# Dealing the second matmul out between single f tiles, transposes behind f tiles 13 and 14, plain tap products and a new ramp, in a fused dynamic convolution and feed-forward kernel

## Chip, cores and metric

One core of one Trainium2 chip. The metric is the device time of one execution in microseconds (us), lower is better. Every run is recorded at a granted clock of 0.993 to 1.000.

## The reference, cut to what matters

```python
w = softmax(weight_gen, axis=-1)                     # (8, 4096, 8 heads, 7 taps)
x_pad = concat([zeros(B, 6, 192), x], axis=1)
out = einsum('bshk,bskhg->bshg', w, windows(x_pad))  # causal, 7 taps, 24 channels a head
h = out.reshape(32768, 192) @ w_in                   # 192 -> 2048
y = (h - tanh(h)) @ w_out                            # 2048 -> 192, float32
```

## The kernel before: the parts that matter

32 blocks (n) of 1024 tokens. For each, GpSimd multiplies the seven taps; an accumulating DMA adds some of the products to others; TensorE (PE) transposes what is left against an identity and sums it in PSUM (`conv_sums`); PE then runs 16 f tiles of the first matmul (`gemm1`; an f tile is 128 of the 2048 hidden columns), ScalarE takes tanh, VectorE (DVE) subtracts, and PE runs the second matmul of the block before (`out_block`, 16 pairs of row tiles for each 128 tokens; a pair is two matmuls on 64 rows each, which overlap in the trace: they start 20 ns apart, pairs 82 ns apart, and each is recorded as 243 ns). `ph`, `pc` and `obank`, which PE writes to, are tiles in PSUM.

```python
for n in range(1, NTOT):
    for p in range(J):                       # J = 8
        more = n < NTOT - 1
        if more and p == 6:
            break
        gemm1(n, 2 * p)
        ...
        gemm1(n, 2 * p + 1)
        ...                                  # softmax pieces of block n + 3
        out_block(n, p, ahead)
        if p == 0 and 1 < n < NTOT - 2:
            products(n + 2, behind=last_sub[0])      # taps of block n + 2, paced
        if p == 0 and n + 3 < NTOT and n not in LATE:
            load_x(n + 3)                            # LATE = (1, ..., 6)
    ...
    gemm1(n, 12); gemm1(n, 13)
    ...                                      # transposes of n + 1 mixed into the pairs of p = 6
    conv_out(n + 1, ((0, 1),), pcs)          # ScalarE
    ...
    conv_out(n + 1, ((2,),), pcs, nc.vector) # DVE
    if n + 3 < NTOT:
        softmax_norm(n + 3, pcs[0][:, 0])    # DVE: copy, scale
    gemm1(n, 14); gemm1(n, 15)
    out_block(n, 7, FILL)
    if n in LATE:
        load_x(n + 3, last_conv[0])          # behind the transposes
```

In `products` each tap is an instruction of its own, the DMA sum follows tap 5 (of taps 0 to 6), and the products lie as [channel third, token, head, 8], so that the transposes load packed columns.

The softmax here doesn't subtract the row's maximum and nothing guards it: scores larger than these inputs give would overflow.

## Time and profile before

| | before |
|---|---|
| median (three runs at the start) | 754.81 us (753.72 to 756.43) |
| busy share PE, DVE, GpSimd, ScalarE | 97%, 93%, 89%, 83% |
| one steady block | 22.49 us |
| loads of x, landing | 1344 KB each, 9.3 us |
| DMA sums, landing | 1024 KB each, 8.8 us |

A busy share averages over stages; what counts is who waits.

### The profile page before, as it was taken

What the parts mean: (1) busy time and instruction counts of PE and PEld (TensorE: products, weight loads), DVE (VectorE), ACT (ScalarE), POOL (GpSimd) and SP (SyncE); (2) the same over time, 40 slices, a digit from 0 to 9 for tenths busy, and PEclk for the clock granted to TensorE, in tenths of its full rate; (3) what the DMA queues carried; (4) which work ended last, traced back from release to release, by engine and by line L of the source; (5) the groups of instructions that cost most, each with busy time, mean ns of one, the idle gap of its engine ahead of it and who ended that gap; (6) DMA issues with size and microseconds to landing.
All of it is one profiled execution on the core that took longest, in us unless ns stands there. A gap on an engine that the chain in (4) does not pass through costs nothing.

```text
span 751.8 us, 32359 instructions
## 1 busy us (share of the span) xinstructions
PE 732.1 (97%) x14800; PEld 577.5 (77%) x14800; DVE 695.5 (93%) x740; ACT 625.3 (83%) x840; POOL 670.5 (89%) x264
## 2 busy tenths in 40 slices
PE   3899999999999999999999999999999999999997
PEld 2477878877777778777777778777878777877777
DVE  7999999999999999999999999999999999998893
ACT  4888888888888888888888888888888888888883
POOL 8999999999999999999999999999999999999000
PEclk9999999999999999999999999999999999999999
DMA  8936444465556665555666544666544566542312
GB/s 229 213 79 172 152 149 111 107 186 171 158 161 155 186 184 126 136 151 160 176 186 172 125 130 149 171 184 186 121 125 148 168 186 173 121 115 62 79 45 86
DMA packets 25943, 110.82 MB, mean 147 GB/s; under 512 B 4703, under 2 KB 9551, under 8 KB 21838
## 3 DMA queue, kind: packets, MB, share of 16 engines
q1 hardware_dynamic: 14718, 77.03, 28.3%
q0 software_dynamic: 11088, 31.72, 24.9%
q8 instruction: 115, 1.88, 1.0%
q14 instruction: 22, 0.18, 0.1%
HBM read 54.52 MB, written 25.17 MB: 106 GB/s over the span
## 4 chain that ended last, share of the span: by engine, by line
PE 94%; DVE 4%; DMA 1%; ACT 0%; issue 0%; DVEq 0%
PE obank L358 44%; PE ph L320 43%; PE pc L277 6%; DVE gt L334 2%; PE po L395 1%; DMA x_t<-in_x_dram 1%; DVE odd L224 0%; DMA wg_t<-in_weight_gen_dram 0%; DVE even L224 0%; DVE zsum L160 0%; DVE obank L199 0%; ACT convT L295 0%; ACT e_t L146 0%; DVE obank L188 0%; DVE zr L169 0%
## 5 line engine op out<-in xcount | busy, mean ns | idle before, releaser
L334 DVE TENSOR_TENSOR gt<-ph,th 128x1024 bf16<-128x1024 f32 x512 | 602.5, 1220 | 33.0 <-ACT th L333 30.0
L333 ACT ACTIVATE th<-ph 128x1024 f32<-128x1024 f32 x512 | 497.5, 1022 | 69.4 <-PE ph L320 68.0
L358 PE MATMUL obank<-w_out,gt 64*128 64x192 bf16 x7936 | 412.5, 243 | 0.1
L358 PEld LDWEIGHTS <-gt 64*128 64x128 bf16 x7936 | 357.4, 94 | 55.7 <-issue 0.2
L320 PE MATMUL ph<-convT,w_in 64*128 64x512 bf16 x3072 | 384.9, 378 | 4.8 <-DVE gt L334 2.8
L224 POOL TENSOR_TENSOR even<-x_t,wsm 128x1536 bf16<-128x1536 f32 x93 | 287.6, 3092 | 12.3 <-DVE gt L334 12.1
L224 POOL TENSOR_TENSOR odd<-x_t,wsm 128x1536 bf16<-128x1536 f32 x93 | 287.3, 3089 | 0.0
L320 PEld LDWEIGHTS <-w_in 64*128 64x128 bf16 x3072 | 174.6, 94 | 101.6 <-issue 11.6
L377 ACT ACTIVATE out_sb<-obank 128x192 f32<-128x192 f32 x248 | 82.3, 332 | 35.0 <-PE obank L358 30.5
L224 POOL TENSOR_TENSOR last<-x_t,wsm 128x1536 bf16<-128x1536 f32 x32 | 106.6, 3333 | 0.0
L277 PE MATMUL pc<-ident,even 64*128 64x64 bf16 x2256 | 62.8, 191 | 0.3 <-DVE even L224 0.2
L277 PEld LDWEIGHTS <-even 64*128 64x128 bf16 x2304 | 59.7, 96 | 1.2 <-issue 0.5
L241 POOL DMA_DIRECT2D even<-odd x30 | 36.1, 1205 | 9.3 <-POOL odd L224 9.3
L277 PE MATMUL pc<-ident,last 64*128 64x64 bf16 x752 | 27.2, 191 | 9.3 <-POOL last L224 9.2
L303 ACT ACTIVATE convT<-pc 128x1024 bf16<-128x1024 f32 (+1 forms) x33 | 32.6, 992 | 2.8 <-PE pc L277 2.8
L277 PEld LDWEIGHTS <-last 64*128 64x128 bf16 x768 | 23.2, 96 | 9.6 <-POOL last L224 9.2
L160 DVE TENSOR_REDUCE zsum<-e_t 128x32 f32<-128x224 f32 (+1 forms) x61 | 23.7, 388 | 3.0 <-ACT e_t L146 3.0
L146 ACT ACTIVATE e_t<-wg_t 128x448 f32<-128x448 f32 x32 | 18.5, 578 | 6.7 <-DMA wg_t<-in_weight_gen_dram 6.7
L301 DVE CAST convT<-pc 128x512 bf16<-128x512 f32 x30 | 20.7, 690 | 3.6 <-PE pc L277 1.9
L169 DVE RECIPROCAL zr<-zsum 128x32 f32<-128x32 f32 (+1 forms) x58 | 20.3, 350 | 0.0
L199 DVE TENSOR_TENSOR wsm<-e_t,pc 128x448 f32<-128x448 f32 x28 | 17.4, 622 | 2.9
L277 PE MATMUL pc<-ident,odd 64*128 64x64 bf16 x416 | 14.7, 198 | 1.1 <-POOL odd L224 0.7
(29 smaller groups left out, 77.5 us busy)
## 6 DMA issues: line engine op xcount, KB each, us to landing
x_t<-in_x_dram SPq DMA_DIRECT2D x31, 1344.0 KB, 9.3
even<-odd POOLq DMA_DIRECT2D x25, 1024.0 KB, 8.8
out_dram<-out_sb SPq DMA_DIRECT2D x31, 768.0 KB, 6.9
wg_t<-in_weight_gen_dram SPq DMA_DIRECT2D x32, 224.0 KB, 10.0
even<-odd POOLq DMA_DIRECT2D x5, 768.0 KB, 7.1
x_t<-in_x_dram SPq DMA_DIRECT2D x1, 768.0 KB
w_out<-in_moe_w_out_dram POOLq DMA_DIRECT2D x1, 768.0 KB, 10.3
out_dram<-out_sb SPq DMA_DIRECT2D x4, 192.0 KB, 1.9
```

Of the source, the lines that this page charges most:

```text
L160: nc.vector.reduce_sum(out=zsum_of[n][:, j0 * H : j1 * H], in_=e_of[n][:, j0:j1].rearrange("p j h k -> p (j h) k"), axis=AX.X,)
L169: nc.vector.reciprocal(zr_of[n][:, j0 * H : j1 * H], zsum_of[n][:, j0 * H : j1 * H])
L224: mul = eng.tensor_mul(dst[k][:, :, j0:j1].rearrange("p c j h g -> p j h c g"), x_t[:, k + j0 : k + j1, :].rearrange("p j (h c g) -> p j h ...
L241: nc.gpsimd.dma_start(out=even[:].rearrange("p i c j h g -> p (i c j h g)")[:, 0:acc], in_=odd[:].rearrange("p i c j h g -> p (i c j h g)" ...
L277: nc.tensor.matmul(pc[r][:, col : col + R] if home else pc[:, r, col : col + R], lhsT=prods[c][gi][r * R : (r + 1) * R, c, 2 * j : 2 * j + ...
L301: eng.tensor_copy(out, pc[:, :, 0:cols].rearrange("p r (cj t) -> p r cj t", t=R))
L303: last_conv[0] = nc.scalar.activation(out=out, in_=pc[:, :, 0:cols].rearrange("p r (cj t) -> p r cj t", t=R), func=ACT.Copy,)
L320: nc.tensor.matmul(ph[:, r, :], lhsT=w_in[r * R : (r + 1) * R, c, f * P : (f + 1) * P], rhs=convT[r * R : (r + 1) * R, c, :], start=(c == ...
L333: last_act[0] = nc.scalar.activation(out=th[:], in_=ph_f, func=ACT.Tanh)
L334: last_sub[0] = nc.vector.tensor_sub(gt[:], ph_f, th[:])
L358: mm = nc.tensor.matmul(po[:, 0:D], lhsT=g_of[n][f][r * R : (r + 1) * R, col : col + P], rhs=w_out[r * R : (r + 1) * R, f, :], start=(r == ...
L377: last_act[0] = nc.scalar.activation(out=out_sb[:, j, :], in_=po[:, 0:D], func=ACT.Copy)
```

## The change

Its intent: keep PE fed at finer grain, take the last eviction from DVE, use fewer GpSimd instructions, need fewer transposes, and close the gap between the first two blocks. The diff, cut to its core:

```diff
-    PART = (2, 3, 4, 5, 6)
+    PART = tuple(range(2,5))
+    SUM_FIRST = tuple(range(5,32))
 ...
-        even = ppool.tile([P, NPAIR, NC, J, H, GC], BF16, name="even")
-        ... odd, last; one instruction per tap
+        pr = ppool.tile([P, K, J, D], BF16, name="pr")
+            mul(nc.gpsimd, 0, 2)
+            mul(nc.gpsimd, 2, 6)
+            if n in SUM_FIRST:
+                dma_sum(pr, 0, 3, 3, 6)
+            mul(nc.gpsimd, 6, K)
 ...
-    (conv_sums) lhsT=prods[c][gi][r * R : (r + 1) * R, c, 2 * j : 2 * j + 2]   # packed
+    (conv_sums) ... "p j (u c) -> p c (j u)" [:, c]                             # step of 3
 ...
+    STEADY = dict(pairs=(4, 12, 0, 16, 0, 16, 0, 16, 0, 6, 10, 6, 10, 8, 8, 16),
+                  t1=(14, 8), t2=(13, 0), scale=14, sums=(2, 5))
+    X_AT = 7
+        for f in range(NFT):
+            gemm1(n, f)
 ...
-                products(n + 2, behind=last_sub[0])
+                    products(n + 2)                      # f == 1, no pace
-            if p == 0 and n + 3 < NTOT and n not in LATE:
-                load_x(n + 3)
+            if f == X_AT and n + 3 < NTOT:
+                load_x(n + 3, last_sub[0])
 ...
+                    pc = transposes(n + 1, chunks)       # in one run; ScalarE evicts
 ...
-    softmax_norm_ramp(2)              # GpSimd scales block 2's weights
+    softmax_norm_ramp(2, obank[0])    # DVE scales them
```

More of the change, by code (lines that the diff above doesn't have):

```diff
@@ L43 @@
     NC = D // R
-    GC = G // NC
-    NPAIR = K // 2
-    ACC = NPAIR * J * D - J * R
     PLAIN = (0, 1)
-    PART = (2, 3, 4, 5, 6)
-    assert S % TOK == 0 and D % R == 0 and H * GC == R and F % P == 0
+    PART = tuple(range(2,5))
+    TWO_SUMS = tuple(())
+    SUM_FIRST = tuple(range(5,32))
+    SCALE_TWICE = True
+    assert S % TOK == 0 and D % R == 0 and F % P == 0
     assert NFT == 2 * J, "one token block of the second matmul per pair of f tiles"
@@ L77 @@
     prods_of = {}
+    to_sum = {}
     conv_of = {}
@@ L174, in softmax_norm, with finish, softmax_norm_ramp @@
         zr_v = bank[:, 512 - J * H : 512]
-        nc.vector.tensor_copy(zr_v, zr_of[n][:])
-        scale(nc.vector, wsm[:], e_of[n], zr_v)
-        wsm_of[n] = (wsm, None, None, None)
-    def softmax_norm_ramp(n, bank=None):
+        nc.vector.reciprocal(zr_v, zsum_of[n][:])
+        def finish():
+            scale(nc.vector, wsm[:], e_of[n], zr_v)
+            wsm_of[n] = (wsm, None, None, None)
+        return finish
+    def softmax_norm_ramp(n, bank):
         softmax_sum(n)
         wsm = softmax_tile()
-        if bank is None:
-            softmax_recip(n)
-            wsm_of[n] = (wsm, None, e_of[n], zr_of[n])
-            return
         zr_v = bank[:, 512 - J * H : 512]
         nc.vector.reciprocal(zr_v, zsum_of[n][:])
-        if n == 0:
+        if n == 2:
             scale(nc.vector, wsm[:], e_of[n], zr_v)
-        else:
-            zr_of[n] = wgpool.tile([P, J * H], FP32, name="zr")
-            nc.vector.tensor_copy(zr_of[n][:], zr_v)
+            wsm_of[n] = (wsm, None, None, None)
+            return
         wsm_v = bank[:, 0 : J * H * K].rearrange("p (j h k) -> p j h k", j=J, h=H)
+        if n == 0 and SCALE_TWICE:
+            scale(nc.vector, wsm[:], e_of[n], zr_v)
         scale(nc.vector, wsm_v, e_of[n], zr_v)
-        wsm_of[n] = (wsm, wsm_v, None if n == 0 else e_of[n], zr_of.get(n))
+        if n == 1 or not SCALE_TWICE:
+            nc.scalar.activation(
+                out=wsm[:].rearrange("p j h k -> p (j h k)"),
+                in_=wsm_v.rearrange("p j h k -> p (j h k)"),
+                func=ACT.Copy,
+            )
+        wsm_of[n] = (wsm, wsm_v, None, None)
     def scale(eng, wsm, e_t, zr):
@@ L203, in scale, with dma_sum, products @@
         )
-    def products(n, taps=None, sums=None, hooks={}, behind=None):
+    def dma_sum(pr, k0, k1, src0, src1, step=1):
+        nc.gpsimd.dma_start(
+            out=pr[:, k0:k1].rearrange("p k j d -> p k (j d)"),
+            in_=pr[:, src0:src1:step].rearrange("p k j d -> p k (j d)"),
+            accum_op=mybir.AluOpType.add,
+            max_dma_last_dim=2 * J * D,
+        )
+    def products(n, taps=None, sums=None, hooks={}):
         x_t = x_of.pop(n)
@@ L210, in products @@
             scale(nc.gpsimd, wsm[:], e_t, zr[:])
-        even = ppool.tile([P, NPAIR, NC, J, H, GC], BF16, name="even")
-        odd = ppool.tile([P, NPAIR, NC, J, H, GC], BF16, name="odd")
-        last = ppool.tile([P, NC, J, H, GC], BF16, name="last")
-        dst = {}
-        for i in range(NPAIR):
-            dst[2 * i] = even[:, i]
-            dst[2 * i + 1] = odd[:, i]
-        dst[K - 1] = last[:]
-        if -1 in hooks:
-            hooks[-1]()
-        for eng, k, j0, j1 in taps or [(nc.gpsimd, k, 0, J) for k in range(K)]:
-            w = wsm_v if eng is nc.vector else wsm[:]
-            mul = eng.tensor_mul(
-                dst[k][:, :, j0:j1].rearrange("p c j h g -> p j h c g"),
-                x_t[:, k + j0 : k + j1, :].rearrange("p j (h c g) -> p j h c g", h=H, c=NC),
-                w[:, j0:j1, :, k : k + 1]
-                .rearrange("p j h (k o) -> p j h k o", o=1)
-                .to_broadcast([P, j1 - j0, H, NC, GC]),
-            )
-            if k == 0 and behind is not None:
-                order(mul, behind, "pace")
-            if j1 == 1:
-                first_halo[0] = mul
-            if (k, n in PART) in ((3, True), (K - 2, False)) and n not in PLAIN:
-                acc = 2 * J * D if n in PART else ACC
-                nc.gpsimd.dma_start(
-                    out=even[:].rearrange("p i c j h g -> p (i c j h g)")[:, 0:acc],
-                    in_=odd[:].rearrange("p i c j h g -> p (i c j h g)")[:, 0:acc],
-                    accum_op=mybir.AluOpType.add,
-                    max_dma_last_dim=4096,
-                )
-            if k in hooks:
-                hooks[k]()
@@ new lines, in products, with mul @@
+        pr = ppool.tile([P, K, J, D], BF16, name="pr")
+        x_v = x_t[:]
+        step = x_v.ap[0]
+        def mul(eng, k0, k1, j0=0, j1=J):
+            w = wsm_v if eng is nc.vector else wsm[:]
+            nj = j1 - j0
+            return eng.tensor_mul(
+                pr[:, k0:k1, j0:j1, :].rearrange("p k j (h g) -> p k (j h) g", h=H),
+                bass.AP(
+                    tensor=x_v.tensor,
+                    offset=x_v.offset + (k0 + j0) * D,
+                    ap=[step, [D, k1 - k0], [G, nj * H], [1, G]],
+                ),
+                w[:, j0:j1]
+                .rearrange("p j h (k o) -> p k (j h) o", o=1)[:, k0:k1]
+                .to_broadcast([P, k1 - k0, nj * H, G]),
+            )
@@ L250, in products, with parts @@
+        def parts(*ks):
+            return [[pr[:, k] for k in ks]] * NC
+        if taps is not None:
+            for eng, k0, k1, j0, j1 in taps:
+                m = mul(eng, k0, k1, j0, j1)
+                if j1 == 1:
+                    first_halo[0] = m
+                if k0 in hooks:
+                    hooks[k0]()
+            prods_of[n] = parts(*sums)
+            return
         if n in PLAIN:
-            prods_of[n] = [[dst[k] for k in (sums or range(K))]] * NC
+            mul(nc.gpsimd, 0, 3)
+            mul(nc.gpsimd, 3, 5)
+            mul(nc.gpsimd, 5, K)
+            prods_of[n] = parts(*range(K))
@@ L252, in products @@
         elif n in PART:
-            prods_of[n] = [[dst[4], even[:, 0], even[:, 1], dst[5], last[:]]] * NC
-        else:
-            groups = [last[:]] + [even[:, i] for i in range(NPAIR)]
-            prods_of[n] = [
-                groups + ([odd[:, NPAIR - 1]] if c == NC - 1 else []) for c in range(NC)
-            ]
+            mul(nc.gpsimd, 0, 2)
+            mul(nc.gpsimd, 2, 4)
+            dma_sum(pr, 0, 2, 2, 4)
+            mul(nc.gpsimd, 4, K)
+            prods_of[n] = parts(4, 5, 6, 0, 1)
+        else:
+            mul(nc.gpsimd, 0, 2)
+            second_sum(n - 1)
+            mul(nc.gpsimd, 2, 6)
+            if n in SUM_FIRST:
+                dma_sum(pr, 0, 3, 3, 6)
+            mul(nc.gpsimd, 6, K)
+            if n not in SUM_FIRST:
+                dma_sum(pr, 0, 3, 3, 6)
+            if n in TWO_SUMS:
+                to_sum[n] = pr
+                prods_of[n] = parts(0, 1)
+            else:
+                prods_of[n] = parts(6, 0, 1, 2)
+            if n == NTOT - 1:
+                second_sum(n)
@@ L260, in conv_sums, with second_sum @@
+    def second_sum(n):
+        if n in to_sum:
+            dma_sum(to_sum.pop(n), 0, 2, 2, K, 4)
     def conv_sums(n, parts, pcs, home=None):
@@ L278, in conv_sums @@
                                 pc[r][:, col : col + R] if home else pc[:, r, col : col + R],
-                                lhsT=prods[c][gi][
-                                    r * R : (r + 1) * R, c, 2 * j : 2 * j + 2
-                                ].rearrange("p j h g -> p (j h g)"),
+                                lhsT=prods[c][gi][r * R : (r + 1) * R, 2 * j : 2 * j + 2].rearrange(
+                                    "p j (u c) -> p c (j u)", c=NC
+                                )[:, c],
                                 rhs=ident[r * R : (r + 1) * R, r * R : (r + 1) * R],
@@ L337 @@
     LAST = (NTOT - 1) * J
-    LEAD = 5
-    FILL, AHEAD = 2, 1
-    LATE = (1, 2, 3, 4, 5, 6)
     half = {}
     out_of = {}
-    def gemm2(i, f0=0, f1=NFT, between=lambda f: None):
-        ops = []
-        for r, blk in ((0, i), (1, i - 1)):
-            if not 0 <= blk < LAST:
-                continue
-            n, j = divmod(blk, J)
-            if r == 0 and f0 == 0:
-                half[blk] = obank[blk % 2]
-            ops.append((r, n, j, half[blk]))
-        for f in range(f0, f1):
-            for r, n, j, po in ops:
-                col = (j % 2) * HT + (j // 2) * P
-                mm = nc.tensor.matmul(
-                    po[:, 0:D],
-                    lhsT=g_of[n][f][r * R : (r + 1) * R, col : col + P],
-                    rhs=w_out[r * R : (r + 1) * R, f, :],
-                    start=(r == 0 and f == 0),
-                    stop=(r == 1 and f == NFT - 1),
-                )
-                if r == 1 and f == 0 and i in (1, LAST):
-                    order(mm, probe[0] if i == 1 else last_act[0], "row tiles in one bank")
-            between(f)
-        if i > 0 and f1 == NFT:
-            blk = i - 1
-            n, j = divmod(blk, J)
-            po = half.pop(blk)
-            if j == 0:
-                out_of[n] = opool.tile([P, J, D], FP32, name="out_sb")
-            out_sb = out_of[n]
-            last_act[0] = nc.scalar.activation(out=out_sb[:, j, :], in_=po[:, 0:D], func=ACT.Copy)
-            if j == J - 1:
-                out_of.pop(n)
-                g_of.pop(n)
-                nc.sync.dma_start(
-                    out=out[n * TOK : (n + 1) * TOK, :].rearrange("(p j) e -> p j e", p=P),
-                    in_=out_sb[:],
-                )
@@ new lines, in out_stream @@
+    def out_stream():
+        for i in range(LAST + 1):
+            ops = []
+            for r, blk in ((0, i), (1, i - 1)):
+                if not 0 <= blk < LAST:
+                    continue
+                n, j = divmod(blk, J)
+                if r == 0:
+                    half[blk] = obank[blk % 2]
+                ops.append((r, n, j, half[blk]))
+            for f in range(NFT):
+                for r, n, j, po in ops:
+                    col = (j % 2) * HT + (j // 2) * P
+                    mm = nc.tensor.matmul(
+                        po[:, 0:D],
+                        lhsT=g_of[n][f][r * R : (r + 1) * R, col : col + P],
+                        rhs=w_out[r * R : (r + 1) * R, f, :],
+                        start=(r == 0 and f == 0),
+                        stop=(r == 1 and f == NFT - 1),
+                    )
+                    if r == 1 and f == 0 and i in (1, LAST):
+                        order(mm, probe[0] if i == 1 else last_act[0], "row tiles in one bank")
+                if f == NFT - 1 and i > 0:
+                    store_out(i - 1)
+                yield
@@ new lines, in store_out @@
+    def store_out(blk):
+        n, j = divmod(blk, J)
+        po = half.pop(blk)
+        if j == 0:
+            out_of[n] = opool.tile([P, J, D], FP32, name="out_sb")
+        out_sb = out_of[n]
+        last_act[0] = nc.scalar.activation(out=out_sb[:, j, :], in_=po[:, 0:D], func=ACT.Copy)
+        if j == J - 1:
+            out_of.pop(n)
+            g_of.pop(n)
+            nc.sync.dma_start(
+                out=out[n * TOK : (n + 1) * TOK, :].rearrange("(p j) e -> p j e", p=P),
+                in_=out_sb[:],
+            )
@@ L386, in gemm2_last, with out_pairs @@
+    pairs = out_stream()
+    def out_pairs(m):
+        for _ in range(m):
+            next(pairs)
     def gemm2_last(j, f0=0, f1=NFT):
@@ L426, with load_w_in @@
     FA = 7 * P
-    def w_in_rows(c, f0, f1):
-        src = moe_w_in[c * GC : c * GC + 1, f0:f1]
-        return bass.AP(
-            tensor=src.tensor, offset=src.offset, ap=[[G * F, H], [F, GC], [1, f1 - f0]]
-        )
-    def load_w_in(f0, f1, behind=None):
-        for c in range(NC):
-            dma = nc.gpsimd.dma_start(out=w_in[0:R, c, f0:f1], in_=w_in_rows(c, f0, f1))
-            if c == 0 and behind is not None:
-                order(dma, behind, "order of the loads")
+    def load_w_in(c0, c1, f0, f1, behind=None):
+        src = moe_w_in[c0 : c0 + 1, f0:f1]
+        dma = nc.gpsimd.dma_start(
+            out=w_in[0:R, c0:c1, f0:f1],
+            in_=bass.AP(
+                tensor=src.tensor,
+                offset=src.offset,
+                ap=[[NC * F, R], [F, c1 - c0], [1, f1 - f0]],
+            ),
+        )
+        if behind is not None:
+            order(dma, behind, "order of the loads")
     def rest_of_w_in():
-        load_w_in(FA, F)
+        load_w_in(0, NC, FA, F)
     V, G_ = nc.vector, nc.gpsimd
@@ L448 @@
     softmax_exp(0)
-    load_w_in(0, FA, last_exp[0])
+    for c in range(NC):
+        load_w_in(c, c + 1, 0, FA, last_exp[0] if c == 0 else None)
     softmax_norm_ramp(0, obank[0])
@@ L454 @@
         taps=[
-            (G_, 6, 0, J),
-            (V, 5, 1, J),
-            (V, 4, 2, J),
-            (V, 5, 0, 1),
-            (V, 4, 0, 2),
-            (G_, 0, 0, J),
-            (V, 3, 0, J),
-            (V, 2, 0, J),
-            (G_, 1, 0, J),
+            (G_, 6, 7, 0, J),
+            (V, 5, 6, 1, J),
+            (V, 4, 5, 2, J),
+            (V, 5, 6, 0, 1),
+            (V, 4, 5, 0, 2),
+            (G_, 0, 1, 0, J),
+            (V, 3, 4, 0, J),
+            (V, 2, 3, 0, J),
+            (G_, 1, 2, 0, J),
         ],
@@ L479 @@
         1,
-        taps=[(V, 0, 0, J), (V, 1, 0, J)] + [(G_, k, 0, J) for k in range(2, K)],
-        hooks={4: load_w_out},
+        taps=[(V, 0, 1, 0, J), (V, 1, 2, 0, J), (G_, 2, 5, 0, J), (G_, 5, 7, 0, J)],
+        sums=range(K),
+        hooks={2: load_w_out},
     )
@@ L494 @@
     load_x(3)
-    for p in range(J):
-        gemm1(0, 2 * p)
-        gemm1(0, 2 * p + 1)
-        if p == 3:
+    PER = 4 * JH
+    EARLY, THIRD = ((7, 3), (9, 1), (11, 7)), 13
+    for f in range(NFT):
+        gemm1(0, f)
+        if f == 1:
+            softmax_exp(3)
+        if f == EARLY[0][0]:
             pcs = []
             sums = conv_sums(1, ((0, 1),), pcs, obank)
-        if p == 0:
-            softmax_exp(3)
-        if 3 <= p <= 6:
-            some(sums, (3 if p == 3 else 1) * 4 * JH)
@@ L507 @@
-    some(sums, K * 4 * JH)
-    conv_out(1, ((0, 1),), pcs)
-    conv(1, (2,))
-    def out_block(n, p, f0=0, f1=NFT, between=lambda f: None):
-        gemm2((n - 1) * J + p, f0, f1, between)
-    for n in range(1, NTOT):
-        for p in range(J):
-            more = n < NTOT - 1
-            if more and p == 6:
-                break
-            gemm1(n, 2 * p)
-            ahead = AHEAD if p == 0 and n > 1 else 0
-            if ahead:
-                out_block(n, p, 0, ahead)
-            gemm1(n, 2 * p + 1)
+        for at, groups in EARLY:
+            if f == at:
+                some(sums, groups * PER)
@@ new lines @@
+        if f == EARLY[-1][0]:
+            conv_out(1, ((0, 1),), pcs)
+        if f == THIRD:
+            pcs = []
+            for _ in conv_sums(1, ((2,),), pcs, obank):
+                pass
+            conv_out(1, ((2,),), pcs)
+    STEADY = dict(pairs=(4, 12, 0, 16, 0, 16, 0, 16, 0, 6, 10, 6, 10, 8, 8, 16), t1=(14, 8), t2=(13, 0), scale=14, sums=(2, 5))
+    FIRST = dict(pairs=(4, 12, 0, 16, 1, 15, 0, 16, 0, 16, 0, 13, 3, 0, 16, 16), t1=(15, 2), t2=(11, 10), scale=15, sums=(1, 2, 3, 4, 8, 10))
@@ L524, with transposes @@
+    X_AT = 7
+    def transposes(n, chunks):
+        pcs = []
+        for _ in conv_sums(n, (chunks,), pcs):
+            pass
+        conv_out(n, (chunks,), pcs)
+        return pcs[0]
+    for n in range(1, NTOT):
+        more = n < NTOT - 1
+        finish = None
+        plan = FIRST if n == 1 else STEADY
+        for f in range(NFT):
+            gemm1(n, f)
             if n == 1:
-                if p == 0:
+                if f == 1:
                     load_wg(5)
-                if p <= 1:
-                    softmax_sum(3, p * JH, (p + 1) * JH)
-                elif p <= 3:
-                    softmax_recip(3, (p - 2) * JH, (p - 1) * JH)
-                else:
-                    softmax_sum(4, (p - 4) * JH, (p - 3) * JH)
@@ L534 @@
-                if p == 2:
-                    softmax_exp(4)
-                if p == 3:
+                if f == 5:
+                    softmax_exp(4)
+                steps = ((softmax_sum, 3), (softmax_recip, 3), (softmax_sum, 4))
+                for at, (step, m, h) in zip(plan["sums"], [s + (h,) for s in steps for h in (0, 1)]):
+                    if f == at:
+                        step(m, h * JH, (h + 1) * JH)
+                if f == 5:
                     wsm_of[3] = (softmax_tile(), None, e_of[3], zr_of[3])
@@ L538 @@
                     products(3)
-            elif n + 3 < NTOT:
-                if p == 0:
+            elif f == 1:
+                if n + 3 < NTOT:
                     softmax_exp(n + 3)
-                if p == 0 and n + 4 < NTOT:
+                if n + 4 < NTOT:
                     load_wg(n + 4)
-                if 1 <= p <= 2:
-                    softmax_sum(n + 3, (p - 1) * JH, p * JH)
-                if 3 <= p <= 4:
-                    softmax_recip(n + 3, (p - 3) * JH, (p - 2) * JH)
@@ L548 @@
-            out_block(n, p, ahead)
-            if p == 0 and 1 < n < NTOT - 2:
-                products(n + 2, behind=last_sub[0])
-            if p == 0 and n + 3 < NTOT and n not in LATE:
-                load_x(n + 3)
-        if not more:
-            continue
-        gemm1(n, 12)
-        gemm1(n, 13)
-        if n == 1:
-            softmax_recip(4)
-        pcs = []
-        sums = conv_sums(n + 1, ((0, 1),), pcs)
-        mix = -(-len(prods_of[n + 1][0]) * 2 * 2 * JH // (NFT - LEAD))
@@ L563 @@
-        out_block(n, 6, between=lambda f: some(sums, mix if f >= LEAD else 0))
-        some(sums, K * 4 * JH)
-        conv_out(n + 1, ((0, 1),), pcs)
-        pcs = []
-        some(conv_sums(n + 1, ((2,),), pcs), K * 4 * JH)
-        out_block(n, 7, 0, FILL)
-        conv_out(n + 1, ((2,),), pcs, nc.vector)
-        if n + 3 < NTOT:
-            softmax_norm(n + 3, pcs[0][:, 0])
-        gemm1(n, 14)
-        gemm1(n, 15)
-        out_block(n, 7, FILL)
-        if n in LATE:
-            load_x(n + 3, last_conv[0])
+                if n < NTOT - 2:
+                    products(n + 2)
@@ new lines @@
+            if n > 1 and n + 3 < NTOT:
+                for h, at in enumerate(plan["sums"]):
+                    if f == at:
+                        softmax_sum(n + 3, h * JH, (h + 1) * JH)
+            if f == X_AT and n + 3 < NTOT:
+                load_x(n + 3, last_sub[0])
+            done = 0
+            for chunks, at in sorted((((0, 1), plan["t2"]), ((2,), plan["t1"])), key=lambda c: c[1]):
+                if more and at[0] == f:
+                    out_pairs(at[1] - done)
+                    done = at[1]
+                    pc = transposes(n + 1, chunks)
+                    if chunks == (2,) and n + 3 < NTOT:
+                        finish = softmax_norm(n + 3, pc[:, 0])
@@ L583 @@
+            if finish is not None and f >= plan["scale"]:
+                finish()
+                finish = None
+            out_pairs(plan["pairs"][f] - done)
     gemm2_last(0, 0, J)
-    gemm2(LAST)
+    out_pairs(NFT)
     gemm2_last(0, J, NFT)
```

## The prediction

> **What bounds the kernel now.** I read the core view first (granted clock 1.000, so no throttling), then the page's chain, then the instructions in order of time over one steady token block, then the busy time by stretch. The chain is TensorE from end to end:
>
> ```profile
> ## 4 chain that ended last, share of the span: by engine, by line
> PE 94%; DVE 4%; DMA 1%; ACT 0%; issue 0%; DVEq 0%
> PE obank L358 44%; PE ph L320 43%; PE pc L277 6%; DVE gt L334 2%; PE po L395 1%; DMA x_t<-in_x_dram 1%; DVE odd L224 0%; DMA wg_t<-in_weight_gen_dram 0%; DVE even L224 0%; DVE zsum L160 0%; DVE obank L199 0%; ACT convT L295 0%; ACT e_t L146 0%; DVE obank L188 0%; DVE zr L169 0%
> ```
>
> L320 is the first matmul, L358 the second, L277 the transposes that also sum the taps. The 4% of DVE and 1% of DMA are the ramp, before about 38 us. Busy shares alone would mislead: DVE shows 93% and GpSimd 89%. The timeline of a steady stretch (start, duration, engine) shows whether PE ever waits:
>
> ```profile
> 407.05 2.90 POOL L224 TENSOR_TENSOR odd<-x_t,wsm 128x1536 bf16<-128x1536 f32 x1
> 409.26 0.37 DVE L160 TENSOR_REDUCE zsum<-e_t 128x32 f32<-128x224 f32 x1
> 409.60 2.36 DVE L334 TENSOR_TENSOR gt<-ph,th 128x1024 bf16<-128x1024 f32 x2
> 409.91 2.90 POOL L224 TENSOR_TENSOR even<-x_t,wsm 128x1536 bf16<-128x1536 f32 x1
> 410.29 1.48 PE L320 MATMUL ph<-convT,w_in 64*128 64x512 bf16 x12
> ...
> 411.16 1.94 ACT L333 ACTIVATE th<-ph 128x1024 f32<-128x1024 f32 x2 [0.32 <-PE ph L320]
> 411.59 1.50 PE L358 MATMUL obank<-w_out,gt 64*128 64x192 bf16 x32
> ...
> 412.91 1.48 PE L320 MATMUL ph<-convT,w_in 64*128 64x512 bf16 x12
> ```
>
> PE starts two f tiles (12 matmuls) at 410.29, 32 matmuls of the second product at 411.59 and the next two f tiles at 412.91: a step of 2.62 us, with no wait on PE. ScalarE waits 0.32 us for PE in each step, so it has slack. Now the transposes and the block's period:
>
> ```profile
> 403.35 0.34 SPq L381 DMA_DIRECT2D out_dram<-out_sb  x1
> ...
> 419.16 0.43 PEld L277 LDWEIGHTS <-even 64*128 64x128 bf16 x24
> ...
> 419.87 0.69 DVE L301 CAST convT<-pc 128x512 bf16<-128x512 f32 x1
> 420.60 0.23 DVE L175 COPY pc<-zr 128x64 f32<-128x64 f32 x1
> ...
> 420.93 0.62 DVE L199 TENSOR_TENSOR wsm<-e_t,pc 128x448 f32<-128x448 f32 x1
> ...
> 425.84 0.34 SPq L381 DMA_DIRECT2D out_dram<-out_sb  x1
> ```
>
> The same store recurs after 425.84 - 403.35 = 22.49 us: one block of 1024 tokens. In a narrower timeline of PE alone the 24 transposes of one group of taps start at 419.19 and the next at 419.54: 0.35 us for 12 pairs of row tiles, 29 ns a pair.
>
> [...] So a block's floor before is 8 x 2.615 + 52 x 0.0292 = 22.44 us of the 22.49 measured: only 0.05 us is loss. [...] The new transposes load weights with a step of 3 bf16 [...]. No row of this trace has a strided weight load. [...] Here taps follow at 2.86 us (407.05, 409.91), 1.86 ns an element[...].
>
> **The change, part by part.**
> - Transposes, on the path. Block 0 and 1 keep 84 pairs and blocks 2 to 4 keep 60. Blocks 5 and 6 go from 60 to 48, blocks 7 to 31 from 52 to 48, since all three channel thirds now have four groups. Saved: 2 x 12 + 25 x 4 = 124 pairs, which fits the instruction lists (496 fewer PE rows, a load and a matmul each, 248 matmuls). 124 x 29.2 ns = **3.6 us**.
> - First and second matmul: the same counts, so the same floor. Dealing the pairs between single f tiles only moves them.
> - DVE, beside PE. Per block it loses the cast (0.69), the copy (0.23) and two half reciprocals (2 x 0.34), and gains one whole reciprocal (0.56, as its row in the ramp): 21.4 busy now, 20.4 then. ScalarE gains the eviction of the third, about 0.6: 19.3 to 19.9 of 22.4. Neither is on the path unless a PSUM slot comes free late.
> - GpSimd, beside PE. The same 7 x 1536 elements in three instructions: at most 7 x 2.86 = 20.0, plus a DMA issue of 1.2: 21.2 of 22.4. It works a block ahead of its use.
> - The DMA sum grows from 1024 to 1152 KB; at 8.8 us to landing now, an estimated 10 then. It is wanted some 11 us later than that: hidden.
> - Ramp. Block 0 is DVE-bound: its 16 subtractions take 18.15 us. DVE now also scales the weights of block 2 before them (+0.62). GpSimd loses two scalings of 1.1 us. Block 1's transposes of the last third move in between f tiles 13 and 14, so the gap at the turn to block 1 closes: DVE idled 1.54 us there (38.22 to 39.76). Net 1.54 - 0.62 = about **0.9 us**.
> - Tail: unchanged, 16.9 us.
>
> Sum: 754.8 - 3.6 - 0.9 = 750.3.
>
> **Do the new waits hold?** Three PSUM slots are shared by ph and pc, so allocation k needs the reader of k-3 done. I worked one block forward by hand from this trace's spacings: f tile 0.647, pair 0.0825, tanh every 0.915, output eviction 0.32, subtraction every 1.14 and its slot free 1.22 after its start, ScalarE starting 0.22 after PE. With t = 0 at f tile 9: f 11 starts at 2.61, its slot is free at 2.49; f 12 3.76 against 3.63; f 13 5.23 against 4.77; the two-third transposes 5.88 against 5.91 (a wait of 0.03); f 14 7.47 against 7.05; the last third 8.78 against 8.37; f 15 9.24 against 8.05 (ScalarE's eviction); next block f 0 11.21 against 10.60; f 1 12.19 against 11.75 (the scale); f 2 13.82 against 12.94; f 3 14.47 against 14.35; f 5 17.09 against 17.03; f 7 19.70 against 19.65; f 9 22.31 against 22.27. So the plan fits with almost no wait, but with margins of 0.04 to 0.13 in about six places. I add 0.7 us in all for such waits: **751.0**.
>
> **The rivals.** (a) *Strided weight loads are slower.* If a pair took about 53 ns [...], 48 x 24 ns = 1.2 us a block, about 35 us in all: 789. Half of that penalty still makes 770. For: nothing here has measured it, and PE has no slack. [...] I give it 9%. (b) *Late slots.* Should DVE or ScalarE run 0.1 us later than I worked out, about three waits of 0.1 come in each block: +9 us, 760, the gain lost. For: the margins. Against: DVE has 2 us and ScalarE 2.5 us free per block. 13%. (c) *GpSimd becomes the bound* because the new shape (inner run 24) costs more. It would need 21.2 to exceed 22.4, 6% more an element; a 10% dearer element would add about 0.8 us a block, 775. Against: the element count is the same and inner runs are longer. 3%. (d) *The ramp stalls* on block 2's taps in block 1 (wanted near 52 us, done near 52 by my sum): +1 us. (e) *A big gain*, over 2%: PE's floor sums to 1536 x 0.2158 + 4096 x 0.0825 + 1644 x 0.0292 = 717 us, to which the start before the first f tile (about 15 us not counted in it) and the DVE-bound first block (about 8) must be added: below 740 is nearly shut out. 2%.
>
> **Range and chances.** The mechanism leaves little play downwards (no losses and a better ramp: 747.5) and more upwards (rival b in part: 757.5). Within 2% is 739.7 to 769.9. Most of (a) and of (c) passes 769.9, which gives slower 0.08; faster 0.02; same 0.90.
>
> **What would show it right or wrong.** A steady block of about 22.37 us between two output stores, 29 ns per transposed pair, PE still over 90% of the chain; GpSimd's seven taps within 20 us; DVE busy near 20.4 a block; PE's first f tile of block 1 about 1 us earlier than 37.79. Wrong would be: transposed pairs over 35 ns (rival a), waits of the first matmul or of the transposes for DVE or ScalarE above 3 us in sum (b), or DVE's scale and PE's transposes waiting for GpSimd (c).

## More of the kernel before

The DMA queues and the waits of the kernel before, for later comparison. In the first, a queue's packets, megabytes and share of the 16 DMA engines' time. In the second, who waited for whom, in us in all, times, and longest; "issue" means that the engine waited for nothing that the profile shows:

```profile
q1 hardware_dynamic: 14718, 77.03, 28.3%
q0 software_dynamic: 11088, 31.72, 24.9%
q8 instruction: 115, 1.88, 1.0%
```

```profile
PEld L320 <- issue: 11.6, 33, 1.1
PEld L358 <- issue: 0.2, 1, 0.2
```

Queue 8 is easily passed over: its packets take 1.0% of the engines' time. 9.7 of the 11.6 us lie in the ramp (before 61 us), where PE waits anyway.

## The result, and the profile after

The changed kernel took **762.87 us** (758.89 to 764.68, four runs) beside 754.42 of the kernel before: ratio 1.0102, 95% interval 1.0073 to 1.0132. The ratios in this document are worked out from the runs of both kernels; they are not quite the ratios of the medians quoted. Predicted were 751.0 and at most 757.5.

First what came as predicted. The busy time of the engines in one undisturbed stretch of 22.4 us; the columns are length, then PE, weight loads, DVE, ScalarE and GpSimd with their instruction counts, the granted clock, the DMA share and GB/s. Before:

```profile
400.00:422.40 22.40, 22.40 (x459) 17.77 (x456) 21.33 (x24) 19.24 (x27) 21.25 (x9) 1.00 0.58 156
```

After:

```profile
400.00:422.40 22.40, 22.40 (x453) 17.59 (x450) 20.36 (x21) 19.82 (x28) 19.83 (x4) 1.00 0.60 162
```

DVE 20.36 (predicted 20.4), ScalarE 19.82 (19.9). The timeline after, over the transposes and up to f tile 13 of the next block:

```profile
399.98 0.83 PE L354 MATMUL ph<-convT,w_in 64*128 64x512 bf16 x6
...
400.63 1.11 PE L311 MATMUL pc<-ident,pr 64*128 64x64 bf16 x64
...
401.56 0.84 PE L389 MATMUL obank<-w_out,gt 64*128 64x192 bf16 x16
...
422.38 0.83 PE L354 MATMUL ph<-convT,w_in 64*128 64x512 bf16 x6
```

32 transposed pairs start at 400.63 and the next work at 401.56: 29 ns a pair, with loads that step by 3 elements, where the packed ones of the kernel before took 29 ns too (0.35 us for 12 pairs). From f tile 13 to f tile 13 are 22.40 us, where 22.37 were predicted.

But not all blocks take that. From the starts of f tile 0 in the trace, the blocks from 4 on of the first profile take 22.40, 22.40, 22.40, 22.96, 22.44, 22.56, 23.17, 22.64, 23.44 us and so on, up to 24.26. The time went into stops. The chain of the changed kernel in order of time, around one of them:

```profile
568.53 1.23 PE ph L354 x11
569.77 0.98 issue
570.75 0.26 PE ph L354
```

PE stops for 0.98 us and waits for nothing that the profile shows. The waits and the DMA queues of the changed kernel, in the form shown above:

```profile
PEld L389 <- issue: 21.1, 49, 1.8
PEld L354 <- issue: 13.4, 38, 1.8
...
PE ph L354 <- issue: 4.6, 7, 1.0
PE obank L389 <- issue: 3.1, 5, 1.6
```

```profile
q1 hardware_dynamic: 14718, 77.03, 27.4%
q0 software_dynamic: 14128, 35.78, 27.1%
q8 instruction: 113, 1.85, 0.9%
```

The "issue" waits of L389, the second matmul's weight loads (L358 before), grew from 0.2 to 21.1 us. Weight loads run beside the matmuls (582.6 and 734.5 us busy in a span of 762.9), so this is not the time that PE lost, which is counted below. From 62 us on, PE's own listed waits are for "issue" alone. Since nothing else explains them, I looked at the queue with 113 packets, which the profile calls "instruction". Each has 16,384 bytes and takes 0.96 us (median). PE runs 29,104 weight loads and matmuls, 256 times 113.7; in the kernel before 29,600, 256 times 115.6, and there the queue has 115 packets. Both fit one packet for 256 of PE's instructions, so I take the queue to carry PE's own program, and call a packet a fetch and 256 instructions a page.

Then I counted loads and matmuls in order of their starts. From block 2 up to the start of block 31, 15 gaps between matmul starts are over 0.34 us in the first profile of the changed kernel, and **all 15 come after the same number modulo 256, 193** (I count the pages from these places; what stands for the 63 missing ahead of the first load, the trace does not show). Each gap ends 1.3 to 1.6 us after the end of a fetch packet. Fetch k (from 0) starts at the earliest when PE has done k + 0.91 pages, and every gap is at the start of page k + 2, where k is the last fetch to end before the gap does. It looks as if PE had one page beyond the one in use and stopped when the fetch of that one started late; the trace shows these times and no more. From block 2 on, 3 of 109 fetches of the kernel before started with more than 0.6 of the page in use gone; in the changed kernel 16 of 106.

What holds them up? The same columns as above, for stretches of 13 to 17, 17 to 20 and 20 to 24 us of block 17 (f tile 13 starts at 16.3 before and 16.4 after, and the transposes begin in the middle one). Block 17 itself has no stop; it shows where the transfers lie. Before:

```profile
412.80:416.80 4.00, 4.00 (x64) 2.88 (x60) 4.00 (x5) 3.32 (x6) 4.00 (x3) 1.00 0.04 13
416.80:419.80 3.00, 3.00 (x142) 2.98 (x139) 2.74 (x3) 2.10 (x4) 3.00 (x2) 1.00 0.26 82
419.80:423.80 4.00, 4.00 (x64) 2.72 (x59) 3.57 (x5) 3.45 (x5) 3.70 (x3) 1.00 0.10 19
```

After:

```profile
419.00:423.00 4.00, 4.00 (x72) 2.99 (x67) 4.00 (x5) 3.62 (x6) 4.00 (x1) 1.00 0.97 341
423.00:426.00 3.00, 3.00 (x109) 2.68 (x108) 2.31 (x2) 2.49 (x4) 2.70 (x3) 1.00 0.27 43
426.00:430.00 4.00, 4.00 (x95) 3.11 (x91) 3.35 (x4) 3.35 (x6) 2.76 (x2) 1.00 1.03 218
```

The DMA share ahead of the transposes went from 0.04 to 0.97 (the load of x, now behind f tile 7) and behind them from 0.10 to 1.03 (the DMA sum, now issued about 4 us earlier in the block, at 17.7 us instead of 21.9, since the taps no longer wait for f tile 1). In between PE uses up instructions fastest: 128 in 0.93 us for the first 64 transposes, against 88 in 2.62 us for two f tiles with their 16 pairs.

So the theory, F in the expectations: **the load of x and the DMA sum keep all DMA engines busy on both sides of the transposes, PE's fetch starts late and PE runs out of instructions.** Rivals: D, the dense transposes alone outrun the fetch; S, PSUM slots come free late; G, GpSimd must run early.

### The profile page after: what moved, and what is told of

Same layout as the page of the kernel before. It is cut to its first block, busy times and chain, and to the rows that moved or that the text cites. A ratio compares the mean times of both kernels' runs of the same rounds, so it can differ in the third digit from the quotient of the medians. Undisturbed runs are those within 1.5% of the kernel's fastest.

```text
span 762.9 us, 31706 instructions
## 1 busy us (share of the span) xinstructions
PE 734.5 (96%) x14552; PEld 582.6 (76%) x14552; DVE 665.8 (87%) x655; ACT 642.5 (84%) x872; POOL 653.2 (86%) x137
## 4 chain that ended last, share of the span: by engine, by line
PE 93%; DVE 3%; issue 1%; DMA 1%; ACT 1%; SPq 0%; DVEq 0%
PE obank L389 43%; PE ph L354 43%; PE pc L311 6%; PE po L432 1%; DVE gt L368 1%; DVE pr L236 1%; DMA x_t<-in_x_dram 1%; ACT th L367 0%; DVE obank L189 0%; DVE zsum L161 0%; ACT convT L329 0%; DVE obank L207 0%; DVE wsm L207 0%; ACT wsm L199 0%; SPq L100 0%
## 5 line engine op out<-in xcount | busy, mean ns | idle before, releaser
L236 POOL TENSOR_TENSOR pr<-x_t,wsm 128x3072 bf16<-128x3072 f32 (+3 forms) x95 | 623.5, 6653 | 37.1 <-DVE wsm L207 25.5
L354 PE MATMUL ph<-convT,w_in 64*128 64x512 bf16 x3072 | 413.7, 379 | 9.0 <-issue 4.6
L389 PEld LDWEIGHTS <-gt 64*128 64x128 bf16 x7936 | 357.8, 94 | 77.4 <-issue 21.1
L389 PE MATMUL obank<-w_out,gt 64*128 64x192 bf16 x7936 | 404.1, 243 | 3.2 <-issue 3.1
L311 PEld LDWEIGHTS <-pr 64*128 64x128 bf16 x3288 | 60.6, 101 | 19.5 <-POOL pr L236 12.2
L311 PE MATMUL pc<-ident,pr 64*128 64x64 bf16 x3120 | 59.3, 193 | 12.4 <-POOL pr L236 12.0
L337 ACT ACTIVATE convT<-pc 128x1024 bf16<-128x1024 f32 (+1 forms) x62 | 50.3, 813 | 1.9 <-PE pc L311 0.7
L214 POOL DMA_DIRECT2D pr<-pr x30 | 38.4, 1281 | 9.2 <-POOL pr L236 9.2
L176 DVE RECIPROCAL pc<-zsum 128x64 f32<-128x64 f32 x28 | 15.4, 551 | 0.3 <-ACT convT L337 0.3
L236 DVE TENSOR_TENSOR pr<-x_t,obank 128x1536 bf16<-128x1536 f32 (+4 forms) x8 | 10.3, 1347 | 2.2 <-DMA x_t<-in_x_dram 1.6
L432 PE MATMUL po<-w_out,gt 64*128 64x192 bf16 x256 | 11.2, 243 | 0.0
L432 PEld LDWEIGHTS <-gt 64*128 64x128 bf16 x256 | 10.8, 93 | 0.0
## 6 DMA issues: line engine op xcount, KB each, us to landing
pr<-pr POOLq DMA_DIRECT2D x27, 1152.0 KB, 10.1
```

The source lines that it names most:

```text
L214: nc.gpsimd.dma_start(out=pr[:, k0:k1].rearrange("p k j d -> p k (j d)"), in_=pr[:, src0:src1:step].rearrange("p k j d -> p k (j d)"), acc ...
L236: return eng.tensor_mul(pr[:, k0:k1, j0:j1, :].rearrange("p k j (h g) -> p k (j h) g", h=H), bass.AP(tensor=x_v.tensor, offset=x_v.offset ...
L311: nc.tensor.matmul(pc[r][:, col : col + R] if home else pc[:, r, col : col + R], lhsT=prods[c][gi][r * R : (r + 1) * R, 2 * j : 2 * j + 2] ...
L337: last_conv[0] = nc.scalar.activation(out=out, in_=pc[:, :, 0:cols].rearrange("p r (cj t) -> p r cj t", t=R), func=ACT.Copy,)
L354: nc.tensor.matmul(ph[:, r, :], lhsT=w_in[r * R : (r + 1) * R, c, f * P : (f + 1) * P], rhs=convT[r * R : (r + 1) * R, c, :], start=(c == ...
L389: mm = nc.tensor.matmul(po[:, 0:D], lhsT=g_of[n][f][r * R : (r + 1) * R, col : col + P], rhs=w_out[r * R : (r + 1) * R, f, :], start=(r == ...
```

## The experiments

Gap sums in this section are the excess over the normal spacing at instruction 192 or 193 modulo 256, from block 2 up to the start of block 31, gaps over 0.225 us. By this count the kernel before has 0.3 us and the changed kernel 10.5 us. (The sums in the expectations were a simpler count, 9.9 us for the changed kernel.)

### No DMA sums

```diff
     def dma_sum(pr, k0, k1, src0, src1, step=1):
+        return
```

> The changed kernel without any of its accumulating DMAs (the output is then wrong on purpose); every PE, DVE and ScalarE instruction stays where it is. Theory F (PE's own instructions come in 16 KB fetches over the same 16 DMA engines, and the DMA sum, which now runs from about 19 us of a block to 3 us of the next, holds those fetches up just after the dense transposes): the PE gaps over 0.3 us from block 1 on, 9.9 us in sum in the changed kernel, fall under 1.5 us, most blocks take 22.40 us, time about 752. Rival D (the dense run of transposes alone outruns the fetch, DMA or not): gaps stay near 8 to 10 us and the time near 762. Rival S (late PSUM slots, my rival b): gaps stay, since no slot is freed earlier.

Measured: 753.97 us (752.79 to 756.07), ratio to the kernel before 0.9996 (0.9978 to 1.0014); wrong result, as meant. Gap sum 1.6 us. Rivals D and S fall: PE's order and every slot are as in the changed kernel.

### The old pace back

```diff
-                    products(n + 2)
+                    products(n + 2, behind=last_sub[0])
...
-            mul(nc.gpsimd, 0, 2)
+            m = mul(nc.gpsimd, 0, 2)
+            if behind is not None:
+                order(m, behind, "pace")
```

> The changed kernel with the old pace put back: GpSimd's first taps of a block wait for the subtraction of f tile 1, so the DMA sum issues some 3.5 us later in the block, near f tile 15, behind the transposes. Theory F: most of the gaps go (under 4 us left of 9.9), time 753 to 757, the rest of the harm being the x load that still ends in the transposes. Rival D: no change, 762. Rival G (GpSimd must run as early as possible): slower than 763.

Measured: 753.75 us (753.01 to 754.97), ratio 0.9987 (0.9970 to 1.0003), gap sum 3.7 us, still all at 193. As expected; rival G falls.

### The load of x two f tiles earlier

```diff
-    X_AT = 7
+    X_AT = 5
```

> The changed kernel with the load of x issued behind f tile 5 instead of 7, about 3 us earlier, so that it ends before the transposes begin; the DMA sum stays where it is. Theory F with the sum as the main culprit: gaps fall only in part, to 5 to 9 us, time 759 to 762. If the x load is the main culprit: gaps under 3 us and 754. Rival D: no change.

Measured: **751.39 us** (750.75 to 751.68), ratio 0.9958 (0.9943 to 0.9972). I had taken the sum for the main culprit, so this is a miss. From block 4 on every block takes 22.40 us (one 22.43), and one gap is left, in block 2. The DMA share over the same three stretches of block 17:

```profile
412.30:416.30 4.00, 4.00 (x72) 3.03 (x68) 4.00 (x5) 3.62 (x6) 4.00 (x1) 1.00 0.39 157
416.30:419.30 3.00, 3.00 (x109) 2.64 (x106) 2.35 (x2) 2.49 (x4) 2.70 (x3) 1.00 0.47 111
419.30:423.30 4.00, 4.00 (x94) 3.13 (x91) 3.32 (x4) 3.35 (x6) 2.75 (x2) 1.00 1.06 184
```

The sum still fills the third stretch, but with the first one freed a page comes in before the transposes, and one of 106 fetches starts with more than 0.6 of the page gone. In this kernel neither transfer does the whole harm alone: it is the pair. (The load of `weight_gen`, 224 KB, is issued behind the load of x on the same queue and moved with it, from 18.6 to 15.9 us into the block. Its share was not tested apart.)

The fetch packets around block 15 show how the two work together; times are from the block's start. In the changed kernel the load of x ends near 18 us, fetch 54 starts at 17.8, the sum runs from 19.5 to 27.5, and fetch 55 starts inside it, at 25.2; a gap of 1.08 us between two matmuls follows. With the early load fetch 54 starts at 15.9 and fetch 55 at 19.3, just ahead of the sum. Without the sums fetch 54 is as late as in the changed kernel (17.9), but fetch 55 starts at 21.3; with the old pace it is 18.0 and 21.9. So the load of x delays one fetch, and only the next one meets the sum.

### Both

> Both: old pace and the load of x behind f tile 5, so that the DMA engines are nearly idle from about 13 us of the block to 22. Theory F: gaps under 1.5 us, blocks at 22.40 us, time 750 to 753, a little faster than the kernel before (ratio 0.994 to 0.999). Rival D: 762.

Measured: 750.98 us (750.43 to 755.23), ratio 0.9966 (0.9938 to 0.9994), gap sum 1.2 us, again the one gap in block 2. The slowest run is the profiled one; in it the full clock came late, 11.9 us after the first f tile, and block 0 took 23.32 us.

### The kernel before, with its two transfers moved

If F holds, moving the two transfers must spoil the kernel **before**, with nothing else changed.

```diff
-                products(n + 2, behind=last_sub[0])
-            if p == 0 and n + 3 < NTOT and n not in LATE:
-                load_x(n + 3)
+                products(n + 2)
+            if p == 3 and n + 3 < NTOT and n not in LATE:
+                load_x(n + 3, last_sub[0])
```

> The kernel BEFORE with only the times of its two big transfers moved to where the change puts them: no pace on GpSimd's taps (the DMA sum then issues near 17 us of a block) and the load of x from block 7 on behind f tile 7 (near 10 to 14 us). No instruction of PE, DVE or ScalarE is moved. Theory F (instruction fetch held up by a load of x and a DMA sum on both sides of the transposes): PE gaps over 0.3 us appear, 3 to 10 us in sum where there was 0.4, all at the same instruction number modulo 256, and the time rises to 757 to 764. Rival: the gaps need the new order of PE's instructions (transposes in two blocks instead of mixed with the second matmul): time stays at 754 to 756 with no gaps.

Measured: **769.85 us** (767.89 to 770.81), ratio 1.0196 (1.0177 to 1.0215), even worse than expected. Gap sum 16.6 us, at 192 or 193 every time. The three stretches of block 17, with the load of x in the first and the sum in the third:

```profile
414.80:418.80 4.00, 4.00 (x64) 2.86 (x60) 4.00 (x5) 3.31 (x6) 4.00 (x2) 1.00 0.99 341
418.80:421.80 3.00, 2.83 (x128) 2.67 (x126) 2.68 (x3) 1.71 (x4) 2.70 (x3) 1.00 0.28 50
421.80:425.80 4.00, 4.00 (x80) 2.88 (x73) 3.27 (x5) 3.48 (x6) 3.58 (x2) 1.00 1.04 223
```

The two parts of it by themselves, first the pace removed, then the load of x moved:

> The kernel before without the pace alone: the DMA sum issues near 17 us of a block, the load of x stays at its old place (4 to 14 us). After the run with both moved (769.9, 12 gaps at one instruction number) and the one with the early load of x in the changed kernel (no gaps from block 3 on), theory F says that it takes both transfers, one ahead of the transposes and one behind them: gaps under 3 us in sum, time 754 to 758. Rival (the DMA sum alone does it): 762 or more.

Measured: 758.11 us (757.64 to 759.02), ratio 1.0048 (1.0031 to 1.0065), gap sum 4.7 us, a little above both bounds set for F, and far below the rival's 762.

> The kernel before with the load of x alone moved behind f tile 7 from block 7 on; the pace stays, so the DMA sum starts in f tile 15. Theory F: gaps of 1 to 5 us in sum, as in the changed kernel with the pace put back (3 us), time 755 to 760. Rival (the load of x alone does it): 765 or more.

Measured: 756.54 us (756.12 to 758.45), ratio 1.0029 (1.0014 to 1.0044), gap sum 2.9 us. The five gaps over 0.34 us show that a fetch need not start late in its page: here 0.26 to 0.37 of the page was gone, against 0.59 or more in the changed kernel. But these pages are dense with transposes and last only 2.5 to 4.5 us, while a fetch takes about 0.95 us and PE goes on 1.3 to 1.6 us after its end. So the dense run (rival D) is not enough by itself, but in these runs it sets how late is too late. Against the kernel before (754.6) the pace alone costs 3.5 us, the load alone 2.0 and both 15.3: they amplify each other, with PE's old order of instructions too.

### The changed kernel again

> The changed kernel unaltered, for a second profile: 759 to 765; gaps of 6 to 11 us in sum at instruction 193 modulo 256, not in the same blocks throughout; the first taps of block 0 start between 6.3 and 8.1 us, which tells whether the 1.8 us by which the first profile began its first f tile later than the kernel before belong to the change or to the run.

Measured: 761.94 us (761.05 to 762.72), ratio 1.0096 (1.0081 to 1.0111), gap sum 9.8 us. The first taps start at 6.07 and the first f tile at 16.66 us, as in the kernel before. In the first profile that was 18.49, so those 1.8 us were chance of that run, and I use this second profile for the balance below.

### The ramp: scaling of block 2 back on GpSimd

In the kernel with the early load of x, block 1 begins 21.39 us after the first f tile, in the kernel before 21.13. A gain was predicted. The trace's clock record shows a difference: full clock is granted for good 4.6 us after the first f tile in the kernel before, and 9.7 us after it there, and PE waited 2.02 us for DVE's first subtraction where it had been 0.60. Ahead of the full clock, f tiles that follow each other without a wait start 1.23 to 1.28 us apart (kernel before and first profile of the changed kernel), in a steady block 0.65: about half the pace. Theory R below lays the late clock to the scaling on DVE.

```diff
-        zr_v = bank[:, 512 - J * H : 512]
-        nc.vector.reciprocal(zr_v, zsum_of[n][:])
         if n == 2:
-            scale(nc.vector, wsm[:], e_of[n], zr_v)
-            wsm_of[n] = (wsm, None, None, None)
+            softmax_recip(n)
+            wsm_of[n] = (wsm, None, e_of[n], zr_of[n])
             return
+        zr_v = bank[:, 512 - J * H : 512]
+        nc.vector.reciprocal(zr_v, zsum_of[n][:])
```

> The kernel with the load of x behind f tile 5 (751.4), and the scaling of block 2's weights put back on GpSimd as in the kernel before, 0.62 us less on DVE ahead of block 0's first subtraction. Theory R (that work kept PE idle [...] and PE at half clock, 1.28 us an f tile, then starves DVE): the full clock is granted within 6 us of the first f tile, block 1 begins about 20.4 instead of 21.4 us after it, time 750.2 to 750.8. Rival (the clock comes late by chance): no change in the clock, 0.3 us or less gained.

Measured: 750.99 us (750.81 to 751.09), ratio 0.9953 (0.9938 to 0.9968). The full clock comes 2.6 us after the first f tile and block 1 begins 20.06 after it, 1.3 us earlier: that half of theory R holds. That PE's waiting is what delays the clock is not shown: here PE waits 1.38 us for DVE's first subtraction, more than in the kernel before, and has the full clock earlier. All profiles agree on the scaling: in the seven with that work on DVE the full clock comes for good 8.5 to 11.9 us after the first f tile, in the six without it (four of them of the kernel before and its variants) 2.6 to 5.8, so chance is a poor rival. But block 1 takes 24.32 us instead of 23.26, and most of the gain is gone. PE's waits of this kernel from 38 to 64 us:

```profile
PE pc L311 <- POOL pr L236: 0.7, 1, 0.7
```

The transposes of block 2 now wait for GpSimd's taps, which end 1.2 us later with the scaling ahead of them; this wait is 0.7 of the 1.06 us, and the rest was not traced. The ramp is held by that chain as well: take one wait away and the next takes its place.

### Block 2's load of x behind its transposes

```diff
-            if f == X_AT and n + 3 < NTOT:
+            if f == X_AT and n + 3 < NTOT and n != 2:
                 load_x(n + 3, last_sub[0])
...
+            if n == 2 and f == NFT - 1:
+                load_x(n + 3, last_conv[0])
```

> The same 751.4 kernel, with the load of x in block 2 alone moved behind block 2's transposes. Theory F: the one gap left (1.1 us in block 2, where that load could not start before 74 us and covers the transposes) goes, block 2 takes 22.8 to 23.0 instead of 24.0 us, time 750.3.

Measured: 750.68 us (750.36 to 753.11), ratio 0.9956 (0.9940 to 0.9973). The gap goes and block 2 takes 22.75 us. Blocks 2 to 30 together take 650.8 us, where the kernel before takes 654.1.

### Both of the last two

> Both of the last two on top of the early load of x: the gains add up, 749.0 to 750.0, the fastest of all, ratio to the kernel before 0.992 to 0.995.

Measured: 751.35 us (750.98 to 751.52), ratio 0.9958 (0.9943 to 0.9972). A miss: the gains don't add up. In its profile block 1 takes 24.91 us, with 0.5 us of waiting for the taps and a stop of 0.9 us for "issue". That stop falls on instruction 193 modulo 256 like the others, so I take it for a late fetch, now in block 1, which the gap sums don't cover. Block 2 takes 22.79. The five kernels with the early load all lie between 750.7 and 751.4, and I don't rank them.

## Why the prediction was wrong, by its own steps

1. **PE is the bound and 124 pairs go: right.** The floor of 22.44 us a block can be read from the trace: a step of 2.615 us, of which 16 pairs of the second matmul take 1.32 (0.0825 each) and six pairs of the first the rest (0.2158 each), and 0.0292 a transposed pair. Undisturbed blocks take 22.40 us against 22.37, and blocks 2 to 30 gain 3.3 us in the kernel whose gaps are gone (654.1 to 650.8); predicted 3.6.
2. **Strided weight loads are as fast as packed ones: right.** No trace had shown one when this was predicted, so it was my estimate alone; measured are 29 ns a pair with a step of 3 bf16, as with packed columns, and rival (a) didn't come. The 53 ns of that rival were a supposition that no run showed, and its sum was loose: 24 ns on all 1644 pairs are 39 us and not 35.
3. **The hand-worked PSUM slots: right.** From 62 us on the profile lists no wait of PE for DVE, ScalarE or GpSimd, and the assumed 0.7 us of slot waits didn't come. The ramp alone holds such waits: 4.3 us for DVE and ScalarE, by the letter more than the 3 us named as a sign of (b), but the kernel before has 5.1 there. Rivals (b) and (c) didn't come.
4. **"The DMA sum ... wanted some 11 us later than that: hidden": this is the step that failed**, together with two parts of the change that the working never named, the new place of `load_x` and the pace that is gone. The size was right (10 us predicted, 10.1 measured to landing), and its *data* are hidden. But the question put to the transfers was only who waits for their data, not what else the DMA engines carry. They also carry the instruction queue, 113 packets of 16,384 bytes. No rival had it, so the range had no room for it. Cost: 9.8 us of gaps in the second profile, 10.5 in the first.
5. **The ramp's -0.9 us: wrong.** In the second profile block 2 begins at 61.24 us, in the kernel before at 60.62: +0.6 instead. DVE's idle time at the turn did shrink (1.54 to 0.47 us), but block 0 takes 21.32 us against 21.13: the extra DVE work, counted as 0.62 us, also came with a later full clock of PE (8.5 to 11.9 us after the first f tile, 2.6 to 5.8 without that work). With it back on GpSimd block 0 takes 20.06. Block 1 takes 23.27 against 22.83, of which PE waits 0.3 us for DVE; the rest was not traced. Rival (d), the taps "wanted near 52 us, done near 52", came only in the two kernels with the scaling on GpSimd.

The balance, from the second profile to the last matmul's start: 756.23 - 747.45 = +8.8 us. Up to block 2 +0.6; blocks 2 to 30 +7.8, which are -3.3 of step 1 (taken over from the kernel without gaps), +9.8 of gaps and about 1.3 of smaller losses that I didn't trace; block 31 and the tail +0.3. The class "within 2%" was right. With the load of x two f tiles earlier the same change takes 751.39, the predicted 751.0; the agreement is partly luck, since the ramp gave less and nothing like the assumed 0.7 us of slot waits came.

**Left open:** why the fetch starts late. That it stands behind the packets of busy queues is a guess: the trace records when a fetch packet starts and not when it was asked for. Nor did I trace why 15 of the 29 blocks from block 2 on have no gap over 0.34 us in the first profile of the changed kernel; the position of a page in the block may play a part.

## What to carry to other kernels

Ask of each large transfer not only who waits for its data, but what else moves beside it: here an instruction queue, 113 packets of 16,384 bytes for PE's 29,104 instructions, used the DMA engines too, and two bursts (DMA share 0.97 and 1.03) on either side of the densest run of instructions went with stops of PE of 9.8 to 10.5 us in all, which the profile lists as waits for nothing ("issue"); moving one burst away left one stop. Gaps that all fall on one instruction number modulo 256 were the mark of it. When a change rearranges instructions, compare the DMA share by stretch of the loop before and after, since moving a load by two tiles was worth more here than the change itself.
